# A two-layer decode block that streams a K/V cache from HBM: one place of scratch memory becomes kept cache, and some filler matmuls go

## The chip, the cores and the metric

The kernel runs on one core of a Trainium2 chip. The metric is the device time in microseconds (us) of one execution; the median of three runs of the kernel before is 2583.88 us (2583.04 to 2585.59).

## The reference

Two layers run one after the other on the same weights and the same cache: attention for one new token of each of two sequences over 32,768 cached positions, then a gated feedforward part. Per layer:

```python
q = (layernorm(x) @ wq)                  # x: 2 x 1 x 512, 32 query heads of 128
scores = q . k_cache * 128 ** -0.5       # k_cache: 2 x 8 x 32768 x 128, each of 8 heads serves 4 query heads
o = softmax(scores) . v_cache            # v_cache: the same shape
x = x + o @ wo
h = gelu(layernorm(x) @ w_gate) * (layernorm(x) @ w_up)   # 512 -> 1792
x = x + h @ w_down                                         # 1792 -> 512
```

All is float32. The two caches together are 537 MB, and each layer needs all of them.

## The kernel before

**Memory as units.** One SBUF tile, `mem`, holds everything that is loaded. It is cut into 108 *units* of 512 floats in each of 128 partitions (256 KB each). For each of the 16 (head, sequence) pairs of a layer, K is 64 units and V is 64 units. A weight matrix comes in pieces: `wq` in 8 pieces of 4 units, `wo` in one of 4 units for each head, the gate and up weights (`gu`) in 4 pieces of 4 and 4 pieces of 3 units, and the down weights (`wd`) in pieces by `WD_SPLIT`, 14 units in all.

**One ordered stream.** All loads go out from the SyncE queue (SP), line L153, in the order in which they will be used. `pump` issues the next load as soon as its place is free in the allocator's books: a place fixed in `plan()`, or the first hole that fits. On the chip the issue waits for the last matmul that reads what was there before. `done(key)` frees a place. In the long middle of a layer, pieces of 32 units rotate through three places.

**The boundary between the layers.** Layer 1 goes through the pairs in reverse order, so the last pair of layer 0 is the first of layer 1. All 64 units of its V stay in memory (`first`, `second` in `values`), and so do the last `KEEPK = 4` pieces of its K: with `K_SPLIT[ORDER[-1]]` before, 4 + 8 + 8 + 8 = 28 units, at units 64 to 91. While V (64), the kept K (28) and `wo` (4 units at 104) are there, units 92 to 107 are left: four *places* of 4 units, at 92, 96, 100 and 104. Through these go, in turn, `gu` (8 loads), `wd` (4 loads) and `wq` of layer 1 (8 loads). The first three `gu` pieces can be loaded ahead; the fourth needs the place of `wo` (104), which is read by the projection L397. After that each load waits for the matmuls of the load four before it. After `wq`, the first two pieces of new K (8 units each) take two of these places each.

**Order of the work on TensorE (PE) there.** Values of the last pair (L376), `combine` (L383, L387), projection (L397), `residual` (L406 to L434), then `feedforward`: 8 gate/up products (L485; the first four, `e = 0`, write tile S, the other four, `e = 1`, write tile T), with `gelu(e)` on ScalarE and VectorE after each half and `hidden(e)` (transposes, L468, and a copy, L469) to turn its result; 4 down products (L475); `residual` again; 8 query products (L289); then scores on the kept K and on the new K (L327). The next K and V pieces of layer 1 are issued as the kept K is used up.

**Fillers.** `warm(n, bank)` (L251) issues n transposes whose result nobody reads. Before, `feedforward` issues 4 after each of the 8 gate/up products and 8 ahead of the second and third down products.

**The end.** In layer 1 the down weights come as `[4, 4, 4, 1, 1]`: 13 rows go through W (L475) and the last one through `finish` (L443), then the result is stored (L447).

Of the kernel before, what the change touches and what calls it, by code (L numbers as in the profile page):

```python
# [38 lines left out]
ORDER = [(g, b) for g in range(HKV) for b in range(NB)]  # L39
PLAIN = [CHUNK, CHUNK]  # L40


K_SPLIT = {ORDER[-1]: [8, 8, 8, 8, 4, 4, 8, 8, 8], ORDER[-2]: [8, 8, 8, 8, 8, 24]}
V_SPLIT = {ORDER[-1]: [32, 16, 8, 4, 4], ORDER[0]: [32, 16, 8, 4, 4]}

WD_SPLIT = [[4, 4, 4, 2], [4, 4, 4, 1, 1]]
KEEPK = 4


def plan():  # L50


    last, before = ORDER[-1], ORDER[-2]
    out = {}

    def put(split, kind, l, pair, spots):
        s = 0
        for n, o in zip(split.get(pair, PLAIN), spots):
            out[kind, l, *pair, s] = o
            s += n  # L60

    put(K_SPLIT, "k", 0, before, [0, 8, 16, 24, 32, 40])
    put(V_SPLIT, "v", 0, before, [64, 0])
    put(K_SPLIT, "k", 0, last, [32, 40, 48, 56, 92, 64, 68, 76, 84])
    put(V_SPLIT, "v", 0, last, [0, 32, 48, 56, 60])
    out["wo", 0, HKV - 1] = out["wo", 1, HKV - 1] = 104
    for i in range(8):
        out["gu", 0, i] = out["wd", 0, i] = out["wq", 1, i] = [92, 96, 100, 104][i % 4]
    put(K_SPLIT, "k", 1, last, [92, 100, 64, 72, 80])
    put(K_SPLIT, "k", 1, before, [84, 92, 100, 64, 72, 0])  # L70
    put(V_SPLIT, "v", 1, before, [32, 64])
    return out

# [23 lines left out]
def block_kernel(ctx: ExitStack, tc: tile.TileContext, x, consts, kt, vt, wq, wo, gu, wd, out):  # L97
# [9 lines left out]
    at = {}  # L107
    stream = deque()
    planned = plan()

    def take(key, n):
# [43 lines left out]
    def get(key, a):  # L155
        if key not in at:
            pump()
        return at[key][1].rearrange("p (a c) -> p a c", a=a)

    def done(key):  # L160
        give(*at.pop(key)[0])
        pump()
# [3 lines left out]
    def pieces(split, g, b):  # L166

        out, s = [], 0
        for n in split.get((g, b), PLAIN):
            out.append((s, n))  # L170
            s += n
        return out
# [5 lines left out]
    def add(key, src, rows, cols):  # L178
        stream.append((key, src, rows, cols))

    def meets(l, n):

        return (l == 0 and n == len(ORDER) - 1), (l == 1 and n == 0)

    for l in range(2):
        for i in range(2 * KC):
            k, v = divmod(i, 2)
            add(("wq", l, i), wq[k, :, v * HALF:(v + 1) * HALF], P, HALF)
        for n, (g, b) in enumerate(orders[l]):
            second = meets(l, n)[1]  # L190
            kp, vp = pieces(K_SPLIT, g, b), pieces(V_SPLIT, g, b)
            for s, m in kp[:-KEEPK] if second else kp:
# [6 lines left out]
        for i in range(2 * KC):  # L199
            n = 2 * FR[i // KC] * FN  # L200
            add(("gu", l, i), gu[o:o + P * n].rearrange("(p c) -> p c", p=P), P, n)
            o += P * n
        o = 0
        for j, m in enumerate(WD_SPLIT[l]):
            add(("wd", l, j), wd[:, o * DM:(o + m) * DM], P, m * DM)
# [34 lines left out]
    A = ps.tile([P, 512], F32, name="A")  # L240
# [4 lines left out]
    def big():  # L245
        return wk.tile([P, 512], F32, name="big")[:, :]

    def warm(n, bank=T[:, 0]):

        for i in range(n):  # L250
            nc.tensor.transpose(bank[:, :P], ident, ident)  # L251

    def small():
        return ps.tile([P, 512], F32, name="small", bufs=2)
# [3 lines left out]
    def spread():  # L258


        sq = wk.tile([P, KC, NB], F32, name="sq", bufs=1)
        nc.vector.tensor_tensor(sq, xin, xin, op=OP.mult)
        m = small()
        nc.tensor.matmul(m[:, :KC * NB], avg, sq.rearrange("p c b -> p (c b)"), start=True, stop=True)
        var = wk.tile([P, 1], F32, name="var", bufs=1)
        nc.vector.tensor_tensor_reduce(sq.rearrange("p c b -> p (c b)"), m[:, :KC * NB], par, 1.0, EPS,
                                       OP.mult, OP.add, var)
        rstd = wk.tile([P, 1], F32, name="rstd")
        nc.gpsimd.tensor_tensor(rstd, var, half, op=OP.pow)
        state["rstd"] = rstd  # L270
# [9 lines left out]
    def window(k, v):  # L280
        return xpad[:, 30 + 32 * k - 2 * v:62 + 32 * k - 2 * v]
# [30 lines left out]
    def scores(l, n, g, b):  # L312
        first, second = meets(l, n)
        mx = wk.tile([P, 2], F32, name="mx", bufs=1)
        parts = pieces(K_SPLIT, g, b)
        kept = [s for s, m in parts[-KEEPK:]] if first or second else []
# [120 lines left out]
    def finish():  # L437

        w = get(("wd", 1, len(WD_SPLIT[1]) - 1), 1)
        (e, t), j = divmod((FD - 1) // 2, 4), (FD - 1) % 2  # L440
# [8 lines left out]
    def feedforward(l):  # L449
        room = big()  # L450
        a, pr = room[:, :FN], room[:, FN:]
        hT = state["hT"] = big().rearrange("p (j r) -> p j r", r=P)
        nj = FN // P
        both = [S, T]

        def gelu(e):
            gt, ut = both[e][:, 0, :FN], both[e][:, 1, :FN]
            nc.scalar.activation(a, gt, AF.Square, scale=cube)
            nc.vector.tensor_scalar(pr, ut, hrr, None, op0=OP.mult)
            nc.vector.scalar_tensor_tensor(a, a, 1.0, gt, op0=OP.add, op1=OP.mult)  # L460
            nc.scalar.activation(a, a, AF.Tanh, scale=root)
            nc.vector.tensor_tensor(pr, pr, gt, op=OP.mult)
            nc.vector.scalar_tensor_tensor(a, a, 1.0, pr, op0=OP.add, op1=OP.mult)

        def hidden(e):
            m = small()
            for j in range(nj):
                nc.tensor.transpose(m[:, j * P:(j + 1) * P], a[:, j * P:(j + 1) * P], ident)  # L468
            nc.vector.tensor_copy(hT[:, nj * e:nj * e + nj, :].rearrange("p j r -> p (j r)"), m[:, :nj * P])  # L469

        def down(j, n, m):
            w = get(("wd", l, j), m)
            for i in range(n, n + m):
                (e, t), q = divmod(i // nj, 4), i % 4
                nc.tensor.matmul(W[32 * q:32 * q + NB, :], hT[:, nj * e + i % nj, 32 * t:32 * t + NB],  # L475
                                 w[:, i - n, :], start=(i < 4), stop=(i + 4 >= tops))
            done(("wd", l, j))

        tops = FD - l
        for i in range(2 * KC):  # L480
            e, k = divmod(i, KC)
            w = get(("gu", l, i), 2 * FR[e])
            for which in range(2):
                for t in range(FR[e]):
                    nc.tensor.matmul(both[e][32 * t:32 * t + 32, which, :FN], window(k, 0),  # L485
                                     w[:, which * FR[e] + t, :], start=(k == 0), stop=(k == KC - 1))
            done(("gu", l, i))
            if i == 0:
                spread()
                rstd = state["rstd"]  # L490
                hrr, cube, root = (wk.tile([P, 1], F32, name=n, bufs=1) for n in ("hrr", "cube", "root"))
                nc.vector.scalar_tensor_tensor(hrr, rstd, 0.5, rstd, op0=OP.mult, op1=OP.mult)
                nc.vector.tensor_scalar(cube, rstd, math.sqrt(0.044715), None, op0=OP.mult)
                nc.vector.tensor_scalar(root, rstd, math.sqrt(2.0 / math.pi), None, op0=OP.mult)
            if i == KC + 1:
                hidden(0)
            if k == KC - 1:
                gelu(e)
            warm(4, A)
        n = 0  # L500
        for j, m in enumerate(WD_SPLIT[l]):
            if n == 4:
                hidden(1)
            if 4 <= n <= 8:
                warm(8, A)
            if n < tops:
                down(j, n, m)
            n += m

    centre()  # L510
    for l in range(2):
        queries(l)
        stage(l, 0)
        for n, (g, b) in enumerate(orders[l]):
            if n % 2 == 0:
                oT = wk.tile([P, REP, NB], F32, name="oT")
            mx = scores(l, n, g, b)
            p, linv = softmax(mx)
            stage(l, n + 1)
            values(l, n, g, b, p)  # L520
            combine(linv, oT, b, 2 if n == len(ORDER) - 1 else 0)
            if n % 2 == 1:
                project(l, g, oT, n == 1, n == len(ORDER) - 1)
        residual()
        feedforward(l)
        if l == 0:
            residual()
# [58 lines left out]
```

## Time and profile before

| what | value |
|---|---|
| median of three runs | 2583.88 us (2583.04 to 2585.59) |
| the profiled execution | 2582.98 us, of which 2581.2 us are its span |
| bytes moved, mean rate over the span | 1106.60 MB, 429 GB/s |
| busy share of the span: PE, weight loads, VectorE, ScalarE | 53%, 15%, 5%, 3% |
| mean granted TensorE clock | 0.744 of full speed |

The span runs from the first to the last instruction; 1.8 us of the profiled execution lie around it. Busy shares are means over the whole span. The boundary between the layers lies between about 1268 and 1400 us of it.

### The profile page before, as it was taken

Reading aid. Unit: us, or ns where it says so; the run is one execution under the profiler, and the core shown is the slowest. Engines: PE = TensorE matmul, PEld = TensorE weight load, DVE = VectorE, ACT = ScalarE, POOL = GpSimd, SP = SyncE. Lnnn points to the kernel's source line nnn. Section 1 sums busy time; section 2 is a strip of 40 time slices with the busy share of each in tenths; the row PEclk is TensorE's granted clock in tenths of the full one; section 3 lists DMA queues with packets and bytes.
Section 4 is the critical chain, followed back from the end, with each engine's and each line's share of the span. In section 5 each row is a group of like instructions: output and inputs, shape, how many; then the busy total and the mean of one; then the engine's idle time right before and its main releaser. Section 6 shows DMA issues by size and latency. Waiting matters only on the chain.

```text
span 2581.2 us, 20377 instructions
## 1 busy us (share of the span) xinstructions
PE 1366.8 (53%) x9528; PEld 399.5 (15%) x9528; DVE 136.1 (5%) x446; ACT 77.5 (3%) x178; POOL 2.6 (0%) x10
## 2 busy tenths in 40 slices
PE   3554545555445544555576455455545544554557
PEld 0111111111111111111132111111111111111113
DVE  0000000000000000000001000000000000000001
ACT  0000000000000000000000000000000000000000
POOL 0000000000000000000000000000000000000000
PEclk7777777667777777777798777777777776777778
DMA  9999999999999999999999999999999999999998
GB/s 423 425 433 437 431 432 433 431 435 431 429 437 432 431 431 436 431 428 428 425 383 430 440 432 432 432 432 436 428 435 433 432 430 437 429 435 431 432 432 355
DMA packets 30756, 1106.60 MB, mean 429 GB/s; under 512 B 3664, under 2 KB 3792, under 8 KB 5200
## 3 DMA queue, kind: packets, MB, share of 16 engines
q1 hardware_dynamic: 30384, 1105.22, 99.5%
q8 instruction: 75, 1.23, 0.2%
q10 hardware_dynamic: 288, 0.08, 0.0%
q14 instruction: 9, 0.07, 0.0%
HBM read 1105.28 MB, written 0.00 MB: 428 GB/s over the span
## 4 chain that ended last, share of the span: by engine, by line
DMA 62%; PE 25%; another core or an unknown queue 11%; ACT 1%; DVE 1%; issue 0%; ACTq 0%; DVEq 0%; SPq 0%
DMA mem<-in_vt 49%; PE A L376 16%; DMA mem<-in_kt 11%; PE S L327 7%; DMA mem<-in_wd 1%; DMA mem<-in_wq 1%; PE W L397 1%; ACT big L383 0%; PE small L387 0%; DMA cst<-in_consts 0%; DMA mem<-in_gu 0%; PE T L351 0%; PE T L251 0%; PE S L485 0%
## 5 line engine op out<-in xcount | busy, mean ns | idle before, releaser
L327 PE MATMUL S<-mem,qpad 128*32 128x512 f32 x4096 | 582.4, 730 | 570.2 <-DMA mem<-in_kt 567.2
L376 PE MATMUL A<-mem,big 128*16 128x512 f32 x4096 | 585.2, 734 | 482.8 <-DMA mem<-in_vt 482.8
L327 PEld LDWEIGHTS S<-mem,qpad 128*32 128x32 f32 x4096 | 153.4, 131 | 987.2 <-issue 825.4
L376 PEld LDWEIGHTS A<-mem,big 128*16 128x16 f32 x4096 | 129.7, 113 | 905.8 <-issue 738.3
L331 DVE TENSOR_REDUCE mx<-S 128x1 f32<-128x512 f32 x64 | 44.2, 691 | 1142.4 <-PE S L327 1142.4
L351 PE MATMUL T<-cst,big 128*128 128x128 f32 x256 | 52.8, 342 | 68.8 <-ACT big L348 38.6
L348 ACT ACTIVATE big<-S,bias 128x512 f32<-128x512 f32 x64 | 43.4, 683 | 1250.6 <-DVE bias L344 1250.6
L392 DVE TENSOR_REDUCE oT<-small 128x4 f32<-128x64 f32 x32 | 7.2, 224 | 1103.2 <-PE small L387 1103.2
L383 ACT ACTIVATE big<-A,linv 128x512 f32<-128x512 f32 x32 | 22.0, 687 | 1157.0 <-PE A L376 1157.0
L352 DVE COPY big<-T 128x512 f32<-128x512 f32 x64 | 44.2, 691 | 92.0 <-PE T L351 92.0
L351 PEld LDWEIGHTS T<-cst,big 128*128 128x128 f32 x256 | 33.9, 168 | 83.5 <-ACT big L348 67.7
L387 PE MATMUL small<-cst,big 128*128 128x128 f32 x128 | 21.0, 287 | 25.1 <-ACT big L383 25.1
L340 PE MATMUL small<-cst,nm 128*128 128x128 f32 x32 | 10.3, 321 | 34.3 <-DVE nm L338 34.3
L289 PE MATMUL small<-mem,xpad 128*32 128x512 f32 x128 | 21.3, 752 | 11.1 <-DMA mem<-in_wq 10.4
L355 PEld LDWEIGHTS small<-cst,ls 128*128 128x128 f32 x128 | 25.7, 280 | 0.0
L355 PE MATMUL small<-cst,ls 128*128 128x4 f32 x128 | 23.4, 288 | 0.0
L387 PEld LDWEIGHTS small<-cst,big 128*128 128x128 f32 x128 | 13.4, 140 | 53.2 <-ACT big L383 53.2
L397 PE MATMUL W<-mem,oT 128*2 128x512 f32 x128 | 16.6, 592 | 4.6 <-DVE oT L392 4.4
L251 PE MATMUL T<-cst 128*128 128x128 f32 x100 | 16.3, 284 | 0.0
L251 PE MATMUL A<-cst 128*128 128x128 f32 x96 | 14.6, 281 | 0.0
L340 PEld LDWEIGHTS small<-cst,nm 128*128 128x128 f32 x32 | 4.2, 133 | 63.3 <-DVE nm L338 59.2
L251 PEld LDWEIGHTS T<-cst 128*128 128x128 f32 x100 | 11.2, 146 | 14.4 <-issue 14.4
(75 smaller groups left out, 144.0 us busy)
## 6 DMA issues: line engine op xcount, KB each, us to landing
mem<-in_kt SPq DMA_DIRECT2D x21, 2048.0 KB, 35.8
mem<-in_wq SPq DMA_DIRECT2D x16, 1024.0 KB, 9.2
mem<-in_wo SPq DMA_DIRECT2D x16, 1024.0 KB, 51.1
mem<-in_vt SPq DMA_DIRECT2D x3, 4096.0 KB, 45.1
mem<-in_kt SPq DMA_DIRECT2D x2, 6144.0 KB, 36.4
mem<-in_gu SPq DMA_DIRECT2D x8, 1024.0 KB, 37.9
mem<-in_vt SPq DMA_DIRECT2D x3, 2048.0 KB, 49.7
mem<-in_vt SPq DMA_DIRECT2D x6, 1024.0 KB, 52.4
```

Source lines behind the costliest of these rows:

```text
L251: nc.tensor.transpose(bank[:, :P], ident, ident)
L289: nc.tensor.matmul(qp[32 * t:32 * t + 32, :], window(k, v), w[:, t, :], start=(i == 0), stop=(i == 2 * KC - 1))
L327: nc.tensor.matmul(S[32 * t:32 * t + 32, u, :], qpad[n % 2][:, 28 - 4 * c:60 - 4 * c], w[:, QUAD * i + t, :], start=(same_u[0] == 8 * u + ...
L331: nc.vector.tensor_reduce(mx[:, u:u + 1], S[:, u, :], axis=AX.X, op=OP.max)
L348: nc.scalar.activation(p[u], S[:, u, :], AF.Exp, bias=bias, scale=SCALE, accum_out=ls[:, u:u + 1])
L351: nc.tensor.transpose(T[:, u, k * P:(k + 1) * P], p[u][:, k * P:(k + 1) * P], ident)
L352: nc.vector.tensor_copy(p[u], T[:, u, :])
L355: nc.tensor.matmul(m[:, :REP], ls[:, u:u + 1].to_broadcast([P, P]), same, start=(u == 0), stop=(u == 1))
L376: nc.tensor.matmul(A[32 * t:32 * t + 16, :], p[u][:, at_p:at_p + 16], w[:, QUAD * i + t, :], start=(j == 0), stop=(j == NU // QUAD - 1))
L383: nc.scalar.activation(md, A, AF.Copy, scale=linv)
L387: nc.tensor.transpose(m[:, c * P:(c + 1) * P], md[:, c * P:(c + 1) * P], ident)
L397: nc.tensor.matmul(W[32 * t:32 * t + NB, :], oT[:, t, :], w[:, t, :], start=first, stop=final)
```

## The change

1. `K_SPLIT` of the last pair becomes `[4, 4, 4, 4, 8, 8, 8, 8, 8, 8]`, so that the last four pieces, which are kept, are 32 units (at 64 to 95) and no longer 28.
2. Between the layers there are three places of 4 units, at 96, 100 and 104. `gu`, `wd` and `wq` of layer 1 go through them in turn as one flow of 20 loads. After them, the first pieces of new K (4 units each) take one place each.
3. `feedforward` issues no filler after the first four gate/up products (`e = 0`), in both layers.
4. The down weights of layer 1 come as `[1, 4, 4, 4, 1]`. `hidden(1)` and the two fillers keep their positions, counted in pieces: ahead of the second piece, and ahead of the second and third.

```diff
-K_SPLIT = {ORDER[-1]: [8, 8, 8, 8, 4, 4, 8, 8, 8], ORDER[-2]: [8, 8, 8, 8, 8, 24]}
+K_SPLIT = {ORDER[-1]: [4, 4, 4, 4, 8, 8, 8, 8, 8, 8], ORDER[-2]: [8, 8, 8, 8, 8, 24]}
...
-WD_SPLIT = [[4, 4, 4, 2], [4, 4, 4, 1, 1]]
+WD_SPLIT = [[4, 4, 4, 2], [1, 4, 4, 4, 1]]
...
-    put(K_SPLIT, "k", 0, last, [32, 40, 48, 56, 92, 64, 68, 76, 84])
+    put(K_SPLIT, "k", 0, last, [32, 36, 40, 44, 48, 56, 64, 72, 80, 88])
...
-    for i in range(8):
-        out["gu", 0, i] = out["wd", 0, i] = out["wq", 1, i] = [92, 96, 100, 104][i % 4]
-    put(K_SPLIT, "k", 1, last, [92, 100, 64, 72, 80])
-    put(K_SPLIT, "k", 1, before, [84, 92, 100, 64, 72, 0])
+    flow = [("gu", 0, i) for i in range(8)] + [("wd", 0, j) for j in range(4)] + [("wq", 1, i) for i in range(8)]
+    for i, key in enumerate(flow):
+        out[key] = [96, 100, 104][i % 3]
+    put(K_SPLIT, "k", 1, last, [104, 96, 100, 64, 72, 80])
+    put(K_SPLIT, "k", 1, before, [88, 96, 64, 72, 80, 0])
...
-            warm(4, A)
+            if e:
+                warm(4, A)
...
-            if n == 4:
+            if j == 1:
                 hidden(1)
-            if 4 <= n <= 8:
+            if 1 <= j <= 2:
                 warm(8, A)
```

## Rows read from the trace of the kernel before

**Rows 1.** The page: span, GB/s in 40 slices, the queue of all loads.

```profile
span 2581.2 us, 20377 instructions
...
GB/s 423 425 433 437 431 432 433 431 435 431 429 437 432 431 431 436 431 428 428 425 383 430 440 432 432 432 432 436 428 435 433 432 430 437 429 435 431 432 432 355
...
q1 hardware_dynamic: 30384, 1105.22, 99.5%
```

**Rows 2.** Windows: stretch, length, busy us per engine, PE clock, DMA share, GB/s.

```profile
1290.00:1296.00 6.00, 4.78 (x37) 2.11 (x35) 0.23 (x1) 1.37 (x3) 0.00 (x0) 1.00 0.57 223
1296.00:1306.00 10.00, 9.01 (x110) 4.85 (x110) 2.59 (x13) 0.98 (x2) 0.55 (x1) 1.00 0.95 326
1306.00:1336.00 30.00, 22.75 (x181) 9.70 (x176) 3.15 (x12) 1.67 (x4) 0.55 (x1) 1.00 1.01 422
1336.00:1346.00 10.00, 7.50 (x64) 2.76 (x66) 0.46 (x3) 0.69 (x1) 0.00 (x0) 1.00 0.99 376
1400.00:2400.00 1000.00, 511.96 (x3501) 144.80 (x3505) 48.68 (x154) 27.06 (x64) 0.00 (x0) 0.73 1.00 433
2568.00:2576.00 8.00, 6.95 (x59) 3.21 (x60) 1.99 (x5) 0.98 (x2) 0.00 (x0) 1.00 0.49 200
```

**Rows 3.** Timeline, PE: last values, projection, first gate/up product.

```profile
1290.80 1.05 PE L376 MATMUL A<-mem,big 128*16 128x512 f32 x8 [0.46 <-DMA mem<-in_vt]
...
1293.63 1.04 PE L397 MATMUL W<-mem,oT 128*2 128x512 f32 x8
...
1296.69 1.07 PE L485 MATMUL S<-mem,xpad 128*32 128x256 f32 x16 [0.16 <-DVE xpad L434]
```

**Rows 4.** Timeline, SP: two gate/up loads and the first new K load go out.

```profile
1294.73 0.33 SPq L153 DMA_DIRECT2D mem<-in_gu  x1
...
1297.79 0.33 SPq L153 DMA_DIRECT2D mem<-in_gu  x1
...
1335.84 0.33 SPq L153 DMA_DIRECT2D mem<-in_kt  x1
```

**Rows 5.** DMA issues at 1268.59, 1294.73, 1297.79, 1302.78, 1304.38, 0.74: size, us to landing.

```profile
mem<-in_gu SPq DMA_DIRECT2D x1, 1024.0 KB, 29.5
...
mem<-in_gu SPq DMA_DIRECT2D x1, 1024.0 KB, 5.9
...
mem<-in_gu SPq DMA_DIRECT2D x1, 768.0 KB, 4.8
...
mem<-in_gu SPq DMA_DIRECT2D x1, 768.0 KB, 6.7
...
mem<-in_wd SPq DMA_DIRECT2D x1, 1024.0 KB, 8.7
...
mem<-in_wq SPq DMA_DIRECT2D x1, 1024.0 KB, 5.1
```

**Rows 6.** Timeline, PE: query products of layer 0 without fillers, at the kernel's start.

```profile
16.06 1.07 PE L289 MATMUL small<-mem,xpad 128*32 128x512 f32 x8 [1.42 <-DMA mem<-in_wq]
18.55 1.94 PE L289 MATMUL small<-mem,xpad 128*32 128x512 f32 x8 [1.43 <-DMA mem<-in_wq]
```

**Rows 7.** Windows around the second and after the last of these.

```profile
14.60:17.10 2.50, 1.08 (x12) 0.16 (x8) 0.00 (x0) 0.00 (x0) 0.00 (x0) 1.00 1.01 423
19.00:25.00 6.00, 4.90 (x24) 0.40 (x16) 0.00 (x0) 0.00 (x0) 0.00 (x0) 0.50 1.17 497
```

**Rows 8.** Timeline, PE: the end, last gate/up product to `finish`.

```profile
2567.92 1.07 PE L485 MATMUL T<-mem,xpad 128*32 128x256 f32 x12
...
2571.42 0.44 PE L468 MATMUL small<-cst,big 128*128 128x128 f32 x2 [0.35 <-DVE big L463]
...
2572.66 1.04 PE L475 MATMUL W<-mem,big 128*2 128x512 f32 x8
...
2574.97 1.88 PE L475 MATMUL W<-mem,big 128*2 128x512 f32 x10 [0.25 <-DMA mem<-in_wd]
2576.78 1.05 PE L443 MATMUL small<-big,mem 128*128 128x2 f32 x8
```

## The prediction, made before the change was run

> **What bounds the kernel now.** I read the page first. All loads of one queue take 99.5% of sixteen DMA engines for the whole span, and 38 of 40 slices move 418 to 440 GB/s; the two low ones are the slice around 1290 to 1355 us (383) and the last (355) [rows 1]. So the kernel is a stream from HBM, and only two things can move the time: fewer bytes, or less time in which the stream runs thin. The busy shares of the engines say nothing here.
>
> Then the windows, to see where it runs thin [rows 2]. Long stretches of a layer give 433 GB/s (1400 to 2400). Against a round 432, a stretch of length t at rate r loses t x (1 - r/432): 1290 to 1296 (223) 2.9 us; 1296 to 1306 (326) 2.5 us; 1306 to 1336 (422) 0.7 us; 1336 to 1346 (376) 1.3 us; together 7.4 us at the boundary between the layers. At the end 2568 to 2576 (200) loses 4.3 us.
>
> Then the timelines of PE and SP and the issues in the first of these stretches, to see why [rows 3 to 5]. The last values run at 1290.80, the projection L397 at 1293.63. The fourth gate/up load stands behind that projection on SP and goes out at 1294.73. The third went out at 1268.59 and lands 29.5 us later, at 1298.1. In 1290 to 1296 the DMA share is 0.57: about half of the engines have finished all that was issued and stand still, while the other half is still working off the third load. The memory is full; nothing can be asked for until PE has finished with the last values. After that the loads follow each other as PE gives places back.
>
> **The change part by part.** One unit is 512 x 4 x 128 bytes = 0.262 MB, four are 1.05 MB.
>
> *Bytes.* Four more units of K stay, so four fewer are loaded in layer 1: 1.05 MB at 433 GB/s is 2.4 us less. This is a matter of counting; nothing hides it, since the stream is the bound. Term -2.4.
>
> *One load less ahead of the stall.* Only two gate/up loads can now go out before the projection, no longer three; the third takes the place of `wo` and goes out at the same 1294.73, for the values, `combine` and projection ahead of it are untouched. The engines therefore stand still from 2.4 us earlier. The half that is ahead loses all of that: 0.5 x 2.4 = 1.2 us of stream. The half that is behind had work until 1298.1; now it runs dry one load earlier, at 1298.1 - 2.45 = 1295.65 (1.05 MB at 428 GB/s), and gets its first bytes about 2.3 us after the issue (an estimate: the first load of the kernel, with nothing ahead of it, takes 5.1 us to land [rows 5], of which 2.4 us are its own bytes, and the remaining 2.7 us divide between start and finish), so about 1297: 0.5 x 1.35 = 0.7. Term +1.9; from +1.2 (only the half ahead loses) to +2.4 (both lose all of it). Note that this nearly eats the term of the bytes: when the stream stops, 108 units are full in both versions, and a unit of kept K merely replaces a unit of gate/up weights.
>
> *Three places, no longer four, for 20 loads.* A place is used again after issue, landing and PE's use of it. Landing took 5.9 us for 4 units and 4.8 us for 3 units where little was queued ahead [rows 5], PE's use 1.07 us [rows 3]. Three places of 4 units carry 3 x 2.45 = 7.35 us of stream and come round in 5.9 + 1.1 = 7.0: just enough. Three of 3 units carry 5.5 and come round in 4.8 + 1.1 = 5.9: 0.4 short, in less than two rounds. On top come the second down product, which has to wait for `gelu(1)`, `hidden(1)` and eight fillers, and the first query product, which has to wait for the residual; with four places that wait had one load more as cover, now it has about 5 us of two loads. I put +1.5. Lower bound 0 (all places come round in time). Upper: the loads at 1302.78 and 1304.38 took 6.7 and 8.7 us to land [rows 5]. The 8.7 is mostly queueing behind three others, so I count the 6.7: rounds of 7.8 us, short by 0.45 in each of five rounds of 4 units and by 2.3 in one and a half rounds of 3 units, +5.7 in all.
>
> The Trainium skill has a price for this ("DMA: Bandwidth & Descriptors", Anatomy of one DMA): a fixed part of some 2.0 us for a transfer beside its bytes at 436 GB/s. By it 1 MB lands after an estimated 4.4 us, three places come round in 5.5 and this term would be 0; the first load here took 5.1 [rows 5], so the trace is dearer than the page.
>
> *New K in single places.* Before, the first new K needs two places and goes out only at 1335.84 [rows 4], more than 5 us behind the last `wq` load, and 1336 to 1346 loses 1.3 us. Now pieces of 4 units follow `wq` through single places. The gap goes, but three places don't carry more than before. Term -1.0, from -1.3 to 0.
>
> *Fillers.* Each of the eight groups of 4 that go is about 0.6 us of PE (half of the 1.2 between L468 and the next L475, with eight between them [rows 8]). In the middle this lets PE give back the second place 0.6 us earlier, but the third product then waits for its load anyway. It frees PE, not the stream: 0 (bounds -0.5 and 0). What the missing cover may cost is the second rival. In layer 1 the first four loads are there in time, and PE meets the fifth about when it lands: 0.
>
> *Down weights 1, 4, 4, 4, 1.* The sum of bytes at the end is the same, so the last one lands when it did. Before, the third piece landed at 2574.9, two single rows behind it; PE took 1.88 us for four rows and one [rows 8], as a single row costs nearly what four side by side do. Now a piece of 4 lands one unit later, +0.6, and PE needs 1.05 for its four rows in place of 1.88: -0.25. The single row at the front lies in PE's wait for `gelu(1)`: `hidden(1)` comes 3.5 us after the last gate/up product, at 2571.42, in both versions. From there PE came to the second product at 2572.66 and, but for a wait of 0.25, would have come to the third at 2574.72 [rows 8]. The third now ends near 2575.7, a little behind the landing of the fourth piece at 2575.5, and the fourth starts there: 2576.75, against 2576.85 before; some 0.2 earlier if PE, rid of fillers, meets the last gate/up load sooner. Term -0.2; bounds -0.4 and +0.3.
>
> *Smaller rows.* 4-unit pieces give 422 where 32-unit ones give 433 [rows 2]; about 3 MB more come in 4s (K of the last pair in both layers): 0.2 us. Term +0.2, 0 to +0.3.
>
> *Sum:* -2.4 + 1.9 + 1.5 - 1.0 + 0 - 0.2 + 0.2 = 0.0. On the profiled execution, 2582.98 us (2581.2 of span and 1.8 around), that is 2583.0; the median is 0.9 above that execution, so I put the median at 2583.9. Bounds of the terms added up: -2.4 + 1.2 - 1.3 - 0.5 - 0.4 = -3.4 and -2.4 + 2.4 + 5.7 + 0.3 + 0.3 = +6.3.
>
> **Rivals.** 0.2%, or 5.2 us, is about what a measurement of this kernel can tell from no change.
>
> *The three places don't carry the stream* (chance 0.18). From 6.25 us between issue and landing (7.35 less 1.1) the flow hangs on its round trip and not on bandwidth. For it: 6.7 us on rows, and 1296 to 1306 at 326 GB/s although four places were in use. Against it: 5.1 and 5.9 us where little was queued. Midway between my +1.5 and the bound +5.7 plus a delay that grows with the idle engines, +4: 2588.
>
> *The clock falls for want of fillers* (0.15). Query products at the start, without fillers, come every 2.5 us like loads; after some of them the clock went from 1.00 to 0.50 (1.2 GHz) and a product took 1.94 us in place of 1.07 [rows 6, 7]. The first half of the gate products will look like that: PE at work about 1 us in 2.5 to 3. If it falls there, products four to six and the fillers between take twice their time, some 3.2 us a piece against 1.9 us of stream, until the clock is back; two pieces late by 1.3, of which three places can't hide any: +2.5, so 2586.5. Against it: the clock is 1.00 from 1290 on [rows 2], and the poor stretch is three products long. The Trainium skill says of this ("TensorE: Matmul & The Clock Gate", HAM oscillation) that matmuls that stop to wait for a DMA each time let the clock swing down; rows 7 agree, and by that rule the answer would be 2586.5.
>
> *The other side: the lost place costs nothing* (0.17). If the half that is behind gets its bytes at once and the places come round in time, what is left is -2.4 + 1.2 - 1.3 - 0.3: -2.8; and if in 1296 to 1306, where four gate/up loads ran at 326 GB/s, the earlier give-back cuts half of the 2.5 us lost, -4.0: 2579.9. It decides from a landing time below 5 us for 3 and 4 units alike. Against it: four places did not get that here.
>
> That the change doesn't keep more K is no rival; the pieces are counted.
>
> **How the numbers follow.** The balance, about no change, 0.50; the rivals 0.18, 0.15, 0.17. The likeliest is 2583.9. Beyond -5.2 us only the tail of the last rival: 0.05. Beyond +5.2: some 0.08 of the first rival, 0.03 of the second, 0.02 of both at once: 0.13. Within: 0.82. For the range, the low end takes the last rival in (2579.9, less 0.5 for the spread of the runs), the high end the first (2588) and half a microsecond: 2579.4 to 2588.6; outside remain about 0.06 below and 0.13 above.
>
> **What would show each step.** Bytes of the load queue 1.05 MB lower. Third gate/up load issued at about 1294.7, landing near 1300.2, first four products 2.5 to 3 us apart. In 1288 to 1297 a rate below the 223 of before. From 1306 to 1340 rates near 420 if the places carry, near 380 if not. No dip to 376 at the first new K. PE clock 1.00 through the gate products, or 0.50 with products of 1.94 us. At the end four rows of about 1.05 us between the last 4-unit piece and L443. Wrong is the prediction if landing times are over 6.5 us all through, or if the stretch from 1290 to 1306 loses less than the 5.4 us of before.

## The result, and the profile after

The changed kernel takes 2591.09 us (median; 2590.07 to 2594.49), the kernel before 2583.73 us beside it. The ratio is 1.0028 (1.0019 to 1.0037): slower by 7.4 us, where no change was forecast and 2588.6 was the upper end. The first rival had the sign, and even its 2588 was too low.

The page of the changed kernel: span, GB/s in 40 slices, the queue of all loads. They answer [rows 1].

```profile
span 2589.3 us, 20316 instructions
...
GB/s 422 432 429 432 435 434 431 434 435 429 431 437 433 435 425 436 433 429 427 401 346 437 433 433 433 433 432 433 432 435 433 432 430 435 434 432 431 433 434 346
...
q1 hardware_dynamic: 30672, 1104.17, 99.2%
```

The queue moved 1.05 MB less, as counted, and took 8.1 us more of span. The two slices with the most loss are 20 and 21 (401 and 346; before, 425 and 383).

The windows of the changed kernel (columns as in [rows 2]: length, busy us of PE, weight loads, VectorE, ScalarE, GpSimd, PE clock, DMA share, GB/s):

```profile
1290.00:1296.00 6.00, 5.46 (x42) 2.16 (x38) 0.23 (x1) 1.07 (x2) 0.00 (x0) 1.00 0.33 138
1296.00:1306.00 10.00, 5.72 (x76) 2.78 (x74) 1.59 (x11) 0.78 (x3) 0.55 (x1) 1.00 0.87 315
1306.00:1336.00 30.00, 21.44 (x166) 9.74 (x170) 4.15 (x15) 2.18 (x5) 0.55 (x1) 0.94 0.95 353
1336.00:1346.00 10.00, 5.49 (x44) 1.73 (x36) 0.00 (x0) 0.00 (x0) 0.00 (x0) 1.00 0.97 381
1346.00:1356.00 10.00, 8.31 (x72) 3.00 (x72) 0.46 (x3) 0.69 (x1) 0.00 (x0) 1.00 0.94 348
1400.00:2400.00 1000.00, 510.91 (x3489) 144.68 (x3485) 49.41 (x155) 27.07 (x64) 0.00 (x0) 0.72 1.00 433
```

Read the last two columns together. The stall is deeper (138 for 223), but the large loss is the next row but one: 30 us at 353 GB/s, where there were 422. The DMA share there is 0.95: engines that look busy carry a sixth less. The Trainium skill ("Perfetto Trace Analysis", Identifying the Most-Contended Engine) says to judge DMA by the bytes it moves, and not by occupancy, which misleads with 16 engines; this row agrees. What the busy engines do is in the last section.

The timeline of PE of the changed kernel (line numbers are one higher than before): the projection, the third to fifth gate/up product, and four query products; in brackets the idle time ahead and what ended it.

```profile
1294.51 1.04 PE L398 MATMUL W<-mem,oT 128*2 128x512 f32 x8
...
1301.23 1.07 PE L486 MATMUL S<-mem,xpad 128*32 128x256 f32 x16 [1.27 <-DMA mem<-in_gu]
1303.71 1.07 PE L486 MATMUL S<-mem,xpad 128*32 128x256 f32 x16 [1.41 <-DMA mem<-in_gu]
1306.74 1.93 PE L486 MATMUL T<-mem,xpad 128*32 128x256 f32 x12 [1.96 <-DMA mem<-in_gu]
...
1338.75 1.07 PE L290 MATMUL small<-mem,xpad 128*32 128x512 f32 x8 [1.37 <-DMA mem<-in_wq]
...
1341.20 1.07 PE L290 MATMUL small<-mem,xpad 128*32 128x512 f32 x8 [0.80 <-DMA mem<-in_wq]
...
1345.20 1.07 PE L290 MATMUL small<-mem,xpad 128*32 128x512 f32 x8 [2.35 <-DMA mem<-in_wq]
...
1347.68 1.06 PE L290 MATMUL small<-mem,xpad 128*32 128x512 f32 x8 [0.82 <-DMA mem<-in_wq]
```

Each of these products but the projection waits for its load, and each load waited for a place that PE gives back: neither side is full. The query products come in steps of 2.5, 4.0 and 2.5 us; a stream at 428 GB/s would bring one every 2.45.

The DMA issues of `wq` in layer 1, of the changed kernel (eight loads between 1321 and 1343 us; number, size, median us from issue to landing):

```profile
mem<-in_wq SPq DMA_DIRECT2D x8, 1024.0 KB, 7.1
```

7.1 us with three places, over the 6.5 that the prediction had named as a sign of being wrong; the six gate/up loads ahead of them landed in 4.2 to 6.7.

Adding to the issue time of each single load its own time to landing gives the moments at which it landed. The stages, so measured (us):

| | before | after | layout_only | four_single | five_places |
|---|---|---|---|---|---|
| fourth gate/up load lands | 1300.63 | 1303.70 | 1302.21 | 1300.84 | 1300.58 |
| from the fourth gate/up load to the last `wq` load | 38.93 | 43.98 | 42.85 | 37.66 | 36.55 |
| from the last `wq` load to 32 units of new K | 20.36 | 21.80 | 23.05 | 19.81 | 19.72 |
| first K of the next pair lands | 1367.30 | 1374.39 | 1372.93 | 1365.69 | 1366.68 |

(The last three kernels are experiments below.) Each column is one execution, and such stages differ between executions. The second row has 38.3 to 41.1 in three other kernels with four places (fillers_only, slow_use_four, down_only) and 43.2 to 44.5 in three others with three (slow_use_three, after_no_gate_fillers, three_keep28): the two groups do not meet, but four places alone spread by 3.5 us, so that a difference of two columns is a rough size. At the next pair's K the change stands at +7.1 us, its 4 units less included; the last load of the kernel lands 7.2 later (2583.27 for 2576.08). Next to nothing (0.1 us) is won or lost in the rest of layer 1 behind it.

The end, timeline of PE of the changed kernel; it answers [rows 8].

```profile
2579.38 1.04 PE L476 MATMUL W<-mem,big 128*2 128x512 f32 x8
...
2581.37 1.04 PE L476 MATMUL W<-mem,big 128*2 128x512 f32 x8
2582.66 1.04 PE L476 MATMUL W<-mem,big 128*2 128x512 f32 x8 [0.25 <-DMA mem<-in_wd]
2583.63 1.05 PE L444 MATMUL small<-big,mem 128*128 128x2 f32 x8
```

Groups of four rows of 1.04 us, the last one waiting 0.25 for its load: as predicted. From the landing of the last load to the issue of the store it is 2.37 us (before 2.70): -0.33. The store itself then took 2.8 us in this execution and 1.4 in that of before, which the change doesn't touch; it took 1.4 in all the other kernels below that end with it.

### The profile page after: what moved, and what is told of

Same layout as the page of the kernel before. It is cut to its first block, busy times and chain, and to the rows that moved or that the text cites. A ratio compares the mean times of both kernels' runs of the same rounds, so it can differ in the third digit from the quotient of the medians.

```text
span 2589.3 us, 20316 instructions
## 1 busy us (share of the span) xinstructions
PE 1367.5 (53%) x9496; PEld 399.0 (15%) x9496; DVE 136.2 (5%) x446; ACT 77.6 (3%) x178; POOL 2.6 (0%) x10
## 4 chain that ended last, share of the span: by engine, by line
DMA 59%; PE 26%; another core or an unknown queue 13%; DVE 1%; ACT 1%; issue 0%; SPq 0%; ACTq 0%; DVEq 0%
DMA mem<-in_vt 45%; PE A L377 16%; DMA mem<-in_kt 11%; PE S L328 8%; DMA mem<-in_gu 1%; DMA mem<-in_wd 1%; DMA mem<-in_wq 1%; PE T L352 0%; PE W L398 0%; ACT big L384 0%; PE small L388 0%; DMA cst<-in_consts 0%; DVE mx L332 0%; ACT big L349 0%
## 5 line engine op out<-in xcount | busy, mean ns | idle before, releaser
L349 ACT ACTIVATION_READ_ACCUMULATOR big<-S,bias 128x1 f32 x64 | 12.5, 196 | 0.0
```

Source lines behind the costliest of these rows:

```text
L349: nc.scalar.activation(p[u], S[:, u, :], AF.Exp, bias=bias, scale=SCALE, accum_out=ls[:, u:u + 1])
```

## The experiments

Ratios are against the kernel before, run beside each.

**layout_only, fillers_only, down_only: the three parts, each alone.** layout_only has parts 1 and 2 of the change (`K_SPLIT`, `plan`), fillers_only part 3, down_only part 4:

```diff
 # fillers_only
-            warm(4, A)
+            if e:
+                warm(4, A)
 # down_only
-WD_SPLIT = [[4, 4, 4, 2], [4, 4, 4, 1, 1]]
+WD_SPLIT = [[4, 4, 4, 2], [1, 4, 4, 4, 1]]
...
```

> Only the layout of the change: 32 units of K kept, three places; fillers and down weights as before. Theory 'places' (the loads between the layers hang on their round trip through three places): nearly the whole slowdown, +6 to +8.5 us against before, 1306 to 1336 at about 355 GB/s. Rival 'clock' (the missing fillers make the gate products slow and the loads behind them late): no more than +3, since the fillers are back, and PE clock 1.00 through the gate products. Rival 'stall' (only the one load less ahead of the projection costs): +0.5, with rates near 420 after 1306.

> Only the fillers after the first four gate/up products removed; four places, 28 units of K. 'Places' and 'stall': within 1 us of before. 'Clock': +2 to +4 us, with gate products of 1.9 us at 1.2 GHz.

> Only the down weights of layer 1 in pieces 1, 4, 4, 4, 1. All theories: -0.3 us (in the changed kernel the store went out 2.37 us after the last load had landed, before 2.70), too little to time; the profile should show about 2.4 us between the last landing and the store.

Measured: layout_only 2589.12 us, 1.0023 (1.0014 to 1.0032); fillers_only 2584.37, 1.0003 (0.9994 to 1.0012); down_only 2583.92, 1.0000 (0.9991 to 1.0009). The layout alone carries the slowdown: 5.6 us over the kernel before beside it, a little less than expected, with an interval that overlaps that of the whole change. down_only stores 2.4 us after the last landing, as expected. Two windows of layout_only:

```profile
1290.00:1296.00 6.00, 4.83 (x37) 2.31 (x36) 0.37 (x2) 1.38 (x3) 0.00 (x0) 1.00 0.41 143
...
1306.00:1336.00 30.00, 22.75 (x158) 10.06 (x158) 3.15 (x12) 1.67 (x4) 0.55 (x1) 0.89 0.97 350
```

The same 350 GB/s with all fillers in place: the missing fillers are not needed for the loss. (Four places aren't always safe either: the profiled execution of down_only, 2586.53 us, has 397 GB/s from 1306 to 1336.) In the table above its fourth gate/up load lands 1302.21 - 1300.63 = 1.6 us late; its projection ran at 1293.32, 0.3 before that of [rows 3], so that 1.9 of it is the stall.

**three_keep28: three places, with 28 units kept.** Layout as in layout_only, but the last K pieces as before and 4 units left unused between the layers:

```diff
-K_SPLIT = {ORDER[-1]: [4, 4, 4, 4, 8, 8, 8, 8, 8, 8], ...
+K_SPLIT = {ORDER[-1]: [4, 4, 4, 4, 8, 8, 4, 4, 8, 8, 8], ...
...
-    put(K_SPLIT, "k", 1, before, [88, 96, 64, 72, 80, 0])
+    put(K_SPLIT, "k", 1, before, [84, 96, 68, 76, 84, 0])
```

> Three places, but 28 units of K kept as before (units 92 to 95 lie idle between the layers); fillers and down weights as before. It differs from the layout of the change by the 4 units of K that it loads again. 'Places': 2.4 us above the run with the layout alone, so about +9.5 against before. 'Stall': +2.9 against before. If the bytes are worth less than their time in the stream, the difference to the run with the layout alone is clearly under 2.4.

Measured: 2604.74 us, 1.0079 (1.0065 to 1.0092). Its windows:

```profile
1306.00:1336.00 30.00, 22.12 (x167) 9.66 (x161) 3.47 (x13) 1.67 (x4) 0.55 (x1) 0.94 0.98 351
...
1356.00:1400.00 44.00, 34.94 (x261) 10.05 (x257) 3.82 (x12) 2.14 (x5) 0.00 (x0) 0.81 0.76 320
```

The first row repeats the loss of three places. The second is a mishap of my placement: the fifth piece of the next pair's K was given units 84 to 91, where the first piece of the same pair lay and had still to be read, and SP issued nothing from 1373 to 1401 us. So its time says nothing of what 4 units of K are worth.

**half_loads: the same 12 units as six places of 2 units.** Does the number of places or their memory decide?

```diff
-        out[key] = [96, 100, 104][i % 3]
+        out[key] = [96, 98, 100, 102, 104, 106][i % 6]
```

with `gu`, `wq` and `wd` cut in halves to match.

> The layout of the change (32 units of K kept, 12 units of scratch) with fillers and down weights as before, but gate/up, down and query weights between the layers come in loads of half the size through six places of 2 units. Theory 'round trip' (the 12 units come round too slowly: a place is given back only when all of it is landed and used): a half place comes back sooner, so the flow is better filled, +2 to +4 us against before in place of the +5.6 of the layout alone. Rival 'cost of each load' (a load that starts on a short queue loses time of its own, some 1 us, whatever its size): more loads, more loss, +8 or more.

Measured: 2589.45 us, 1.0021 (1.0012 to 1.0030): between the two expectations, and no better than layout_only's ratio. Its window 1306 to 1336 moves 381 GB/s, 1346 to 1356 only 352, at clock 1.00. But it doesn't answer the question, for it changes PE's work too:

```profile
1336.00:1346.00 10.00, 10.00 (x48) 2.69 (x48) 0.00 (x0) 0.00 (x0) 0.00 (x0) 1.00 1.00 367
```

PE is busy 10.00 of 10.00 us. A query product of half a load takes 1.05 us, as one of a whole load does, and with two fillers behind it PE needs 1.35 us for each half megabyte, which alone allows no more than an estimated 0.524 MB / 1.35 us = 388 GB/s. Whether the number of places or their memory decides stays open.

**five_places and four_single: the other direction.** five_places keeps 24 units of K and has five places; four_single keeps before's 28 and four places, but takes the first new K in pieces of 4 units through single places (and has the new down weights).

```diff
 # five_places
-KEEPK = 4
+KEEPK = 3
...
-        out[key] = [96, 100, 104][i % 3]
+        out[key] = [88, 92, 96, 100, 104][i % 5]
...
 # four_single, against the kernel before
-    put(K_SPLIT, "k", 1, last, [92, 100, 64, 72, 80])
+    put(K_SPLIT, "k", 1, last, [92, 96, 100, 104, 64, 72, 80])
...
```

> The other way: 24 units of K kept, five places of 4 units, new K in single places; fillers and down weights as before. 'Round trip': bytes +2.4, one load more ahead of the projection -1.9 to -2.4, 1306 to 1346 at 425 GB/s or more in place of 422 and 376, -1 to -2; in all -1.5 to +0.5 us against before. If the number of places did not matter beyond three, it would be +2.4 from the bytes less 1.9.

> As before with four places and 28 units kept and all fillers, but the first 16 units of new K come as four loads of 4 units, each into one place, and the down weights of layer 1 as 1, 4, 4, 4, 1. With four places the single loads should take away the 376 GB/s of 1336 to 1346: -1 to -1.6 us against before. If single places don't help even here, the step 'new K in single places' of the prediction was wrong by itself and not for want of the fourth place: 0 or slower.

Measured: five_places 2583.17 us, 0.9994 (0.9985 to 1.0003); four_single 2582.33, 0.9993 (0.9985 to 1.0002). Two windows of five_places:

```profile
1290.00:1296.00 6.00, 4.76 (x37) 2.09 (x34) 0.23 (x1) 1.38 (x3) 0.00 (x0) 1.00 0.79 309
...
1306.00:1336.00 30.00, 23.47 (x181) 9.92 (x182) 3.16 (x12) 1.67 (x4) 0.55 (x1) 1.00 1.01 421
```

and one of four_single:

```profile
1336.00:1346.00 10.00, 8.26 (x68) 2.90 (x72) 0.46 (x3) 0.69 (x1) 0.00 (x0) 1.00 1.01 420
```

A fifth place fills the stall (309 for 223); it adds nothing to the flow from 1306 to 1336, where four already gave 422. That the bytes it costs take the gain back fits the ratio near 1, and isn't shown apart from it. In four_single the dip at the first new K is gone (420 for 376). From the last `wq` load to 32 units of new K it needs 19.8 us, where before has 20.4 and the three other kernels with four places 20.8 to 21.0: 0.6 to 1.2 less, about the 1.0 that I had put on single places. The ratio of the whole kernel can't tell this from no change.

**after_no_gate_fillers: the changed kernel with no filler after any gate/up product.** If the clock were the cause, this must be worse.

```diff
-            if e:
-                warm(4, A)
```

> The changed kernel without the fillers after the second four gate/up products too. 'Clock': the clock falls in the gate products and does not come back, products of 1.9 us, +2 to +4 us against the changed kernel, +9 to +11 against before. 'Places' alone: within 1 us of the changed kernel, since PE has time to spare.

Measured: 2589.72 us, 1.0025 (1.0016 to 1.0033). Its timeline of PE, the fourth to sixth gate/up product:

```profile
1303.42 1.94 PE L486 MATMUL S<-mem,xpad 128*32 128x256 f32 x16 [2.75 <-DMA mem<-in_gu]
1305.97 3.75 PE L486 MATMUL T<-mem,xpad 128*32 128x256 f32 x24 [0.61 <-DMA mem<-in_gu]
```

Here three products run at half the clock (1.2 GHz: 1.94 in place of 1.07 us), and the kernel isn't slower than the change. In fillers_only, with four places, the same products took 1.06 to 1.07 us, so that run says nothing of the clock. The clock falls; it doesn't decide.

**slow_use_three and slow_use_four: a longer use of each place.** Each query product of layer 1 is issued a second time into a tile that nobody reads, in place of its four fillers, so that PE holds every `wq` place about 1 us longer; once with three places (layout_only), once with four (before).

```diff
+            if l:
+                for t in range(4):
+                    nc.tensor.matmul(T[32 * t:32 * t + 32, 0, :], window(k, v), w[:, t, :], start=True, stop=True)
             done(("wq", l, i))
...
-            if l:
-                warm(4)
```

> The layout of the change alone (three places), but each query product of layer 1 is issued a second time into a tile that nobody reads, in place of the four fillers behind it, and only then is its place given back: about 1.0 us more use of each place, PE some 2.1 us in each 2.45. Theory 'round trip': the flow hangs on issue, landing and use, so 8 loads through 3 places lose about 1 us in each of 2.7 rounds, +2.5 to +3 us against the run with the layout alone. Rival 'slow loads' (loads of 4 units between the layers are slower in themselves, wherever the place comes back): no difference, within 0.5 us.

> The kernel before (four places, 28 units of K) with the same doubled query products. 'Round trip': four places have some 2 us to spare in each round, so 0 to +0.7 us against before. If the longer use costs here what it costs with three places, it is PE and not the round trip that it slows.

Measured: with three places 2590.79 us, 1.0025 (1.0016 to 1.0033), with four 2583.96, 1.0001 (0.9992 to 1.0010). Against the kernel before beside it, layout_only lost 5.6 us and this one 6.4: 0.9 more, with ratios that can't be told apart, and not the +2.5 to +3 of the round trip. The other expectation, no difference, came nearer. That three places pass a longer use on is not shown; with four, the window 1306 to 1336 keeps 418 GB/s. What the run with three places does show is that the loss is there at full clock:

```profile
1306.00:1336.00 30.00, 22.19 (x186) 9.18 (x190) 4.47 (x16) 2.18 (x5) 0.55 (x1) 1.00 0.94 357
```

**five_down: five_places with the new down weights.**

> The candidate: five places, 24 units of K kept, new K in single places, down weights of layer 1 as 1, 4, 4, 4, 1, all fillers. From the run with five places (-0.06%) and the earlier store (-0.3 us): -1 to -2 us against before, -7 to -9 against the changed kernel.

Measured: 2582.74 us, 0.9994 (0.9985 to 1.0002). Against the changed kernel both this and four_single are some 8 us better; against the kernel before neither is told apart from no change.

**probe: the flow by itself.** In a single execution, behind the store of the kernel before, groups of 16 loads of 4 units go through 1 to 4 places, without a use and with one (four matmuls as in a query product, and four fillers). Nobody reads the results.

```diff
+    def probe(places, uses, count=16, size=4):
+        for i in range(count):
+            o = 56 + size * (i % places)
+            w = mem[:, o * UNIT:(o + size) * UNIT]
+            nc.sync.dma_start(w, wq[i % KC, :, :size * UNIT])
+            for u in range(uses):
...
+            if uses:
+                warm(4, A)
+    for places, uses in ((1, 0), (2, 0), (3, 0), (4, 0), (2, 1), (3, 1), (4, 1), (3, 2), (4, 2)):
+        probe(places, uses)
+    probe(6, 0, 32, 2)
+    probe(6, 1, 32, 2)
```

> The kernel before, and after its result is stored, the disputed flow by itself: groups of 16 loads of 4 units (rows of 8 KB, as the query weights) through 1, 2, 3 or 4 places in turn, without any use by PE, then with one use (four products and four fillers) or two, and 32 loads of 2 units through six places. Only the time from load to load in each group counts. 'Round trip' with the landing time on a short queue (5 to 6 us) and a use of 1.1: one place 5 to 6 us a load, two 2.6 to 3, three and four 2.45 without use; with one use two places 3.1 to 3.5, three 2.45. Rival 'the queue itself needs depth': three places give 2.8 to 3.0 even without a use, four 2.5, and six places of half the size no better than three.

Measured, mean us from landing to landing from the fifth load of each group on:

| places | no use | one use | two uses |
|---|---|---|---|
| 1 | 5.07 | | |
| 2 | 2.99 | 3.2 | |
| 3 | 2.48 | 3.05 | 2.9 |
| 4 | 2.49 | 2.6 | 2.6 |

For three places neither expectation came. 'Round trip' had 2.45 for three places with one use, and a longer use doesn't make it worse (2.9 with two). Its rival wanted three places to fall short even without a use, and they don't.

Half loads through six places take 2.55 us per MB without a use and 3.3 with one. But a use here is the same work for half the bytes, and PE is busy throughout, so that the 3.3 is PE's and says nothing of the places:

```profile
3080.00:3130.00 50.00, 50.00 (x360) 17.92 (x360) 0.00 (x0) 0.00 (x0) 0.00 (x0) 0.94 0.86 300
```

The whole run took 3134.45 us.

The windows of the probe for three places without a use, three with one, four with one:

```profile
2720.00:2745.00 25.00, 0.00 (x0) 0.00 (x0) 0.00 (x0) 0.00 (x0) 0.00 (x0) 0.50 1.01 424
...
2855.00:2890.00 35.00, 23.80 (x144) 7.96 (x144) 0.00 (x0) 0.00 (x0) 0.00 (x0) 0.85 0.96 362
2910.00:2940.00 30.00, 21.73 (x140) 7.59 (x136) 0.00 (x0) 0.00 (x0) 0.00 (x0) 0.89 1.01 421
```

and its timeline of PE for three places with one use:

```profile
2857.90 1.07 PE L539 MATMUL T<-mem,xpad 128*32 128x512 f32 x8 [0.84 <-DMA mem<-in_wq]
...
2861.42 1.07 PE L539 MATMUL T<-mem,xpad 128*32 128x512 f32 x8 [1.87 <-DMA mem<-in_wq]
...
2863.91 1.07 PE L539 MATMUL T<-mem,xpad 128*32 128x512 f32 x8 [0.84 <-DMA mem<-in_wq]
...
2866.36 1.07 PE L539 MATMUL T<-mem,xpad 128*32 128x512 f32 x8 [0.80 <-DMA mem<-in_wq]
...
2870.71 1.77 PE L539 MATMUL T<-mem,xpad 128*32 128x512 f32 x8 [2.69 <-DMA mem<-in_wq]
```

The picture of the changed kernel again, outside it: 362 GB/s at a share of 0.96, steps of 2.5, and once in a while 3.5 to 4.75. The first four of these uses take 1.07 us each, so the clock isn't needed for it. Three places carry the whole stream when the place is free on landing, and not when PE holds it for about 1.1 us first; four carry it nearly, even with two uses, with which PE is busy all the time (34.00 of 34.00 us from 2998 to 3032).

## Why the prediction was wrong

**The step that failed** is the term "three places, no longer four, for 20 loads": +1.5 put, bounds 0 and +5.7, measured 43.98 - 38.93 = +5.05 in this pair of executions and 42.85 - 38.93 = +3.9 in layout_only. That the places might not keep up was written down; the size was wrong. I took 5.9 us for the landing, from a load that had gone out into a nearly empty queue, and so a round of 7.0, "just enough". In the flow the landing is 7.1; with 1.1 of use and a tenth on either side of it a place comes round in 8.4, and single places do so in 7.4 to 9.0 (the last of the three is issued at 1325.09, 1334.07 and 1342.33 us). Three loads at 428 GB/s are 7.35. The term's bound of +5.7 held, but four of six rounds were longer than the 7.8 us behind it.

Nor is the sum of landing and use the mechanism. By it three places with one use would give 2.45 us a load, where the probe has 3.05, and a second use would make it longer, where the probe has 2.9. And no landing time of before would have told the size: its eight `wq` loads took 8.5 us, but four places that share a full stream give each load just that (4 x 2.48 less 1.3 of use and issue). What is shown is narrower: with four places the flow is full, with three and any use by PE it is not.

**New K in single places** fell with it: -1.0 put, bounds -1.3 and 0, measured 21.80 - 20.36 = +1.4, outside its bounds: those four loads go through the same three places (landings at 1350.13, 1354.13, 1356.61 and 1359.29). Where there are four places the step is about right (four_single). The two terms together were put at +0.5 and came to +6.5, and to +6.6 in layout_only, so that their sum is firmer than their parts; that is most of the miss.

**One load less ahead of the stall**, +1.9 (1.2 to 2.4): measured +1.9 in layout_only, and 1303.70 - 1300.63 = +3.1 in the changed kernel, whose projection ran at 1294.51, 0.9 after [rows 3], for a reason of its own (below). Without that 0.9 it is 2.2; the term holds, in part by luck. Its estimate of 2.3 us from issue to first bytes is not borne out: in the probe the first packet of a lone load starts 0.96 us after the issue, and then the engines are slow for a while (last section).

**Bytes**, -2.4: right. From 32 units of new K to the next pair's first piece it is 7.38 us before, over 12 units, and 4.91 after, over 8: -2.5.

**Fillers**, 0: right; fillers_only has 1.0003, with an interval on both sides of 1. The clock did fall for one product (1.93 us), as the rival said; after_no_gate_fillers makes it three products at no visible cost, so the rival's price is refuted, not the fall of the clock. The Trainium skill's rule of the prediction ("TensorE: Matmul & The Clock Gate", HAM oscillation) is borne out by these products. The lost time is caught up soon: in the changed kernel the sixth product starts 1.1 us after its load has landed and the eighth 0.1, and in after_no_gate_fillers the seventh waits 0.89 for its load again.

**Down weights**, -0.2: measured -0.33. **Smaller rows**, +0.2: not told apart. Those of layer 0 lie ahead of the stall, where the second gate/up load lands at 1295.64 before, 1295.84 after and 1295.36 in layout_only; those of layer 1 are inside the new K.

**The sum by what was measured**: 3.1 + 5.05 + 1.4 - 2.5 - 0.3 = +6.7 up to the store; the profiled spans differ by 8.1 with the 1.4 of the store, which no other profiled execution shows, and the medians by 7.4. The upper end of the range, 2588.6, was the first rival's price and half a microsecond; the bounds added up went to 2590.2, and 2591.09 lies above these too, since the new K left its bounds and 0.9 came from elsewhere. (Of the readings, the 38 slices lie between 423 and 440 GB/s, and not from 418 on; nothing hangs on it.) The changed kernel is 1.4 us above after_no_gate_fillers and 2.0 above layout_only; whether that is more than such medians differ by isn't settled.

**The rivals**: "the three places don't carry the stream" (0.18) named what happened, from landings over 6.25 us on, and its +4 was too little. "The lost place costs nothing" needed landings below 5 us; those of `wq` were 7.1. Its half, that four units of kept K are worth 2.4 us, is true and was never enough.

**What stays open** is why three places with a use need 3.05 us for a load, where the sum 5.1 (a load alone) and 1.1 (use), over three, is 2.1 and the stream would allow 2.48. For two places the same sum is near with a use (6.2 / 2 = 3.1 against 3.2) and fails without one (5.07 / 2 = 2.5 against 2.99). For three with a use, landing takes 6.6 to 8.2 us in the settled part although little can be queued ahead. The clock is excluded (357 GB/s at clock 1.00) and so are the missing fillers; the size of the loads is not. Part of it is that the engines are slow after each pause, as the last section shows; what starts the pauses was not found.

## What to carry to other kernels

When a place in memory is given back by the engine that uses it, don't add up the flow from a landing time. The one from an empty queue leaves out what happens in the flow, and the one from a full flow (7.4 us in the probe's three places without a use) is mostly waiting behind the other loads. Measure the flow with its number of places and its use, as the probe does: here three places of 1 MB gave 353 GB/s, four 422, and five no more. Before a buffer is turned into cache, price both ends per unit: four more units of kept K saved 2.5 us, and the place that they took cost 6.5 on the 24 loads that went through the places, and 2 more at the stall. And read the bytes of a stretch, not the busy share of the DMA engines.

## What the hardware showed that I had not expected

The flow through three places with a use runs at much the same rate wherever it was measured: from 1306 to 1336 us 350 to 357 GB/s in the five kernels with three places of 4 units, at a DMA share of 0.94 to 0.98, and 362 GB/s at 0.96 in the probe.

Engines that start again after a pause are busy, but slow. The probe's group with one place shows it by itself; the rows are from the end of one load and the start of the next, which was issued at 2618.07 us:

```profile
2616.00:2617.00 1.00, 0.00 (x0) 0.00 (x0) 0.00 (x0) 0.00 (x0) 0.00 (x0) 0.50 0.99 418
2619.00:2620.00 1.00, 0.00 (x0) 0.00 (x0) 0.00 (x0) 0.00 (x0) 0.00 (x0) 0.50 1.04 213
```

Half the rate at a full share. By the packet records of that load its first sixteen packets of 8 KB took 0.72 us each, the next sixteen 0.48, the last forty-eight 0.31. Such slow packets mark the flow through three places: of the 8 KB packets that start between 1318 and 1345 us, 0.1% took over 0.4 us before and in five_places, 7.5% in the changed kernel and 9.9% in layout_only (4.4% in that execution of down_only); in the probe, three places without a use have 0.0%, with one use 9.0%, and four with one use 0.1%. So a pause costs more than its own length, and this is how busy engines carry a sixth less. That it makes up all of the loss is not shown.

A 1 MB load with nothing else under way took 5.07 us on the mean (4.9 to 5.2) in the probe's group with one place. The Trainium skill's sum ("DMA: Bandwidth & Descriptors", Anatomy of one DMA: about 2.0 us fixed and the bytes at 436 GB/s; it is given for loads issued from GpSimd) makes an estimated 4.4 of it; the measurement, with loads issued from SP, decides.

Ahead of the stall the changed kernel lost 0.9 us at one place, where PE paused and then ran in part at half the clock. Its timeline of PE, values of the last pair:

```profile
1281.18 5.32 PE L377 MATMUL A<-mem,big 128*16 128x512 f32 x32 [2.84 <-DMA mem<-in_vt]
```

and its window there:

```profile
1281.20:1286.50 5.30, 5.30 (x33) 1.18 (x34) 0.00 (x0) 0.00 (x0) 0.00 (x0) 0.68 1.00 419
```

In the kernel before the same 32 matmuls took 3.63 us behind a pause of 1.51, at clock 1.00. layout_only, with the same layout as the changed kernel, ran this place at 1.00 too, so it is no part of the change. That the longer pause brought the clock down was not tested.
